# When the first layer's transfers are let go: pauses moved from POOL to DVE, key loads moved out of the norms' stages

## The chip, the cores and the metric

The kernel runs on one core of a Trainium2 chip. The core has five engines that run side by side, each its own list of instructions in order: PE (matrix products; its weight loads have their own row, PEld), DVE (element-wise work and reductions), ACT (activations and copies), POOL (further element-wise work) and SP, which here only issues DMA transfers. Engines wait for each other, and for transfers, through semaphores. The time that counts is the device time of one execution in microseconds, the median of several.

## The reference, cut to what matters

Two blocks follow each other: a delta-rule attention over 4 batches, 8 heads, 768 steps and 48 dimensions, and a feed-forward layer with a parametric ReLU over the 3072 tokens.

```python
k_n = k / (np.linalg.norm(k, axis=-1, keepdims=True) + 1e-06)
for t in range(S):
    kt, vt, bt = (k_n[:, :, t], v[:, :, t], beta[:, :, t, None])
    y[:, :, t] = np.einsum('bhd,bhde->bhe', q[:, :, t], state)
    v_old = np.einsum('bhde,bhd->bhe', state, kt)
    state = state + bt[:, :, :, None] * np.einsum('bhd,bhe->bhde', kt, vt - v_old)
...
x = np.ascontiguousarray(attn_out.transpose(0, 2, 1, 3)).reshape(B * S, H * D)
h = x @ w_in                                        # 3072 x 384 times 384 x 2048
g = np.maximum(h, 0.0) + alpha * np.minimum(h, 0.0)
return (g @ w_out).astype(np.float32)               # 3072 x 2048 times 2048 x 384
```

## The kernel before

**Steps.** The 768 positions are cut into 12 chunks of 64. A step n is one chunk of one pair of batches, so there are 24 steps; steps 2c and 2c + 1 are chunk c. Inside a step the recurrence over 64 positions becomes small products of 64 x 48 blocks: the Gram products of the keys (`grams`, L495), the triangular system they give, which steps 0 to 3 solve in rounds (`matrix`, `own_values`, `one_round`, all through L866) and later steps with an inverse made by elimination on DVE (`eliminate`), the outputs (`outputs`, L939) and the state's update (`next_state`, L955 and L963). `to_ffn` transposes a step's output (L978), and when both steps of a chunk are done the chunk goes through the two products of the feed-forward layer, first layer `ffn_in` (L1084, with ACT L1094 and DVE L1096 making the activation), second layer `ffn_out` (L1127).

**Weights.** Both weight matrices come as 8-byte numbers and are made into 4-byte ones on the chip, by the generator `weights` (from L203). `w_in` comes in 12 pieces of 128 x 512 numbers, 512 KB each. For a piece, SP issues the transfer into a staging area (L230), ACT makes two halves (L247, L249; `begin_half`), DVE shifts (L263) and POOL adds (L270). `begin_in(n)` has ACT begin all pieces up to n. The staging areas of pieces 0 to 5 lie in `w_out`, of 6 and 7 in `space_out`, 8 and 9 in `more`, 10 in `sums`, 11 in `turned`. The conversion fetches only the first four pieces by itself (`STAGED` is 4). Every later one is let go by a *pause*: a memset of one element of its staging area by some engine, for which SP must wait before it issues the transfer. So the pause's place in that engine's list sets the earliest time of the transfer:

```python
def pause(n, engine=nc.gpsimd):
    engine.memset(in_stages[n][0:1, 0:1].bitcast(FP32), 0.0)
    fetch_in(n + 1)
```

`pause_out` (L1697) does the same for the 128-row pieces of `w_out`, and `hold_v` (L165) lets a load of values wait for two one-element memsets of POOL.

**Keys.** `load_early(n)` (through L137) brings the keys of step n into one of three buffers; it can go when the earlier step in that buffer has been flipped (PE, L439) and squared (ACT, L395). `squared`, then `norms` (DVE, L402), `root` (ACT, L417 and L418), the reciprocal (DVE, L422) and two products of POOL (L428, L429) give a step's weights; all that follows the norms is `weigh`.

**Order.** The whole order is written out by hand: what a function emits goes to the end of its engine's list at that moment. The part around the change is `second_pair` (from L1814): it solves steps 2 and 3 (n and m, chunk 1), runs the first layer for chunk 0 beside it, converts the pieces of `w_in` from the fourth on and the first of `w_out`, and prepares the keys, norms and Grams of steps 4 to 7 (x is 4). `alongside(p, c)` mixes p parts of the first layer (a part is one 128-column product, two PE instructions) with c parts of the conversion (two to a piece). `burst(step, width)` emits a step of the solution for both n and m at once. The other places it names are `through_state` (L816, L804, then DVE L824 and L517), `turn_matrix` and `turn_values` (POOL, L882), `scale_first` (L854, by DVE for n and POOL for m), the weighting of the Grams by DVE (L503) and POOL's copy of part of it (L538).

Of the kernel before, what the change touches and what calls it, by code (L numbers as in the profile page):

```python
# [39 lines left out]
STAGED = 4  # L40
# [3 lines left out]
def kernel(  # L44
# [11 lines left out]
    nc = tc.nc  # L56
# [19 lines left out]
    def ps_big():  # L76

        big.append(big.pop(0))
        return big[-1]
# [24 lines left out]
    def half(i):  # L104
        return slice(64 * i, 64 * i + 64)

    def dims(i):
        return slice(64 * i, 64 * i + D)
# [14 lines left out]
    NKE, NKL, NQ = 3, 2, 2  # L123
# [5 lines left out]
    def early(n):  # L129

        return k_late[1] if n == NKE else k_early[n % NKE]

    def fetch(a, n, dst, queues=(nc.sync, nc.sync)):
        c, bp = steps[n]
        for t in range(2):
            src = a[2 * bp + t, :, c * C : (c + 1) * C, :].rearrange("h p d -> p h d")
            queues[t].dma_start(out=dst[half(t)], in_=src)  # L137

    def load_early(n, *queues):
        if n < N:  # L140
            fetch(k, n, early(n)[:, :, 0:D], *queues)
# [19 lines left out]
    def hold_v(n, engine=nc.gpsimd):  # L161

        v_raw[n] = work.tile([128, H, D], FP32, name="v_raw", bufs=3)
        for t in range(2):
            engine.memset(v_raw[n][64 * t : 64 * t + 1, 0, 0:1], 0.0)  # L165

    def load_v(n):
        if n < N:
            if n not in v_raw:
                v_raw[n] = work.tile([128, H, D], FP32, name="v_raw", bufs=3)  # L170
            fetch(v, n, v_raw[n])
# [237 lines left out]
    def weigh(n):  # L409
        if n >= N:  # L410
            return []
        norm = stats[n]
        root(norm)
        return [lambda: weigh_rest(n, norm)]

    def root(norm):
        nc.scalar.sqrt(norm, norm)  # L417
        nc.scalar.activation(norm, norm, ACT.Copy, bias=1e-6)  # L418

    def weigh_rest(n, norm):  # L420
        rec = work.tile([128, H], FP32, name="rec")
        nc.vector.reciprocal(rec, norm)  # L422
        weights_of(n, norm, rec)
# [48 lines left out]
    def quarters():  # L472
        return [(g, a, t) for g in range(G) for a in range(2) for t in range(2)]

    def now(pieces):
        for x in pieces:
            x()

    def region(p, n, **into):

        p = ps_big()[:, :, 0:n] if p is None else p
        assert p.shape[-1] == n
        return p.rearrange("p a (g i) -> p a g i", **into)

    def grams(n, p=None, u=0):

        if n >= N:
            return []
        if n < NJ:
            p = p.rearrange("p a (g u i) -> p a g u i", g=G, u=2)[:, :, :, u]  # L490
        else:
            p = region(p, G * C, g=G)
        for g, a, t in quarters():
            own = half(t ^ a) if n < NJ else half(t)
            nc.tensor.matmul(  # L495
                p[own, a, g], k_t[n][dims(a), g, half(t)], k_t[n][dims(a), g, half(t)]
            )
        if n < NJ:
            return p

        def weighted(dst, cols):
            w = stats[n][1][:, 0:2, :, None].to_broadcast([128, 2, G, HB])
            nc.vector.tensor_tensor(  # L503
                out=dst.rearrange("p (a g) i -> p a g i", a=2), in0=p[:, :, :, cols], in1=w,
                op=ALU.mult,
            )

        return [
            lambda: weighted(gather(n), slice(0, HB)),
            lambda: weighted(right[n % EARLY][:, 1:], slice(HB, C)),  # L510
            lambda: keep(n),
        ]
# [13 lines left out]
    def gather(n):  # L526
        m, j = n // NJ, n % NJ
        if j == 0:
            same[m] = work.tile([128, NJ, H, HB], FP32, name="same", bufs=1)
        return same[m][:, j]  # L530

    def keep(n):

        m, j = n // NJ, n % NJ
        for t in range(2):
            own = slice(64 * t + HB, 64 * t + C)
            if n < FIRST + NJ:
                nc.gpsimd.tensor_copy(out=same[m][own, j], in_=right[n % EARLY][own, 1:])  # L538
            else:
                nc.scalar.copy(same[m][own, j], right[n % EARLY][own, 1:])  # L540
# [901 lines left out]
    def part(gen, n):  # L1442
        for _ in range(n):
            next(gen, None)
            yield

    def weave(*gens):

        live = []
        for i, (g, n, *at) in enumerate(gens):  # L1450
            at = at[0] if at else 0.0
            live.append([at, i, (1.0 - at) / n, g])
        while live:
            live.sort(key=lambda x: (x[0], x[1]))
            at = live[0]
            at[0] += at[2]
            try:
                next(at[3])
            except StopIteration:
                live.pop(0)  # L1460
# [208 lines left out]
    n = 2 * W_IN_P  # L1669
# [13 lines left out]
# [4 lines that stand above are left out]
# [8 lines left out]
    def pause_out(n, engine=nc.vector):  # L1695

        engine.memset(out_stages[n][0:1, 0:1].bitcast(FP32), 0.0)  # L1697
        fetch_out(n + 1)
# [111 lines left out]
    def alongside(products, pieces, *gens):  # L1810
        gens = [(part(first_in, products), products), (part(convert_on, pieces), pieces), *gens]
        weave(*[x for x in gens if x[1] > 0])

    def second_pair():  # L1814

        n, m, x = 2, 3, NJ
        both = (n, m)

        def burst(step, width):
            p = ps_big()  # L1820
            pieces = []
            for i in range(2):
                pieces += step(n + i, p[:, :, i * width : (i + 1) * width])
            now(pieces)

        def keys(k):
            if k == x + 3:
                flip_more(k)
            squared(k)
            norms(k)  # L1830
            load_early(k + NKE)

        def through(i, p):
            now(through_state(i, None, p))

        now(next_state(0))
        hold_v(n)
        load_v(n)
        pause(STAGED + 2)
        alongside(2, 2)  # L1840
        now(next_state(1))
        keys(x)
        load_v(m)
        pause(STAGED + 3)
        alongside(3, 2)
        pause(STAGED + 4)
        burst(matrix, G * C)
        for i in both:
            turn_matrix(i, nc.gpsimd)
        now(weigh(x))  # L1850
        alongside(3, 2)
        scale_first(n, nc.vector)
        pause(STAGED + 5)
        scale_first(m)
        alongside(2, 0)
        keys(x + 1)
        begin_in(STAGED + 3)
        alongside(2, 1)
        y = ps_big()
        through(n, y[:, :, 0 : G * D])  # L1860
        alongside(2, 1)
        through(m, y[:, :, G * D : 2 * G * D])
        now(weigh(x + 1))
        pause(STAGED + 6)
        begin_in(STAGED + 4)
        alongside(2, 1)
        now(grams(x))
        begin_in(STAGED + 5)
        alongside(2, 2)
        ahead[0] = FT * DM  # L1870
        pause(STAGED + 7)
        burst(own_values, G * D)
        for i in both:
            turn_values(i, nc.gpsimd)
        alongside(2, 1)
        keys(x + 2)
        pause_out(0, nc.gpsimd)
        alongside(2, 2)
        pause_out(1, nc.gpsimd)
        now(grams(x + 1))  # L1880
        alongside(2, 1)
        burst(lambda i, p: one_round(i, 0, p), G * D)
        pause_out(2, nc.gpsimd)
        now(weigh(x + 2))
        alongside(2, 1)
        keys(x + 3)
        alongside(2, 1)
        now(grams(x + 2))
        alongside(2, 2)
        burst(lambda i, p: one_round(i, 1, p), G * D)  # L1890
        pause_out(3)
        now(weigh(x + 3))
        alongside(2, 1)
        now(grams(x + 3))
        alongside(2, 1)
        pause_out(4)
        burst(lambda i, p: one_round(i, 2, p), G * D)
        pause_out(5)
        alongside(3, 3, (part(blocks, 2), 2))
        burst(outputs, G * D)  # L1900
        pause_out(6)
        alongside(4, 3)
        for i in both:
            to_ffn(i)
        squares(x + 4)
        alongside(2, 1, (part(blocks, 2), 2))
        alongside(IN_PARTS - 43, 0, (part(blocks, 2), 2))

    def flip_more(n):
        now(flipped(n, ps_one()))  # L1910
# [21 lines left out]
    n = WHOLE + PIECES - BEGUN - SOON  # L1932
# [28 lines left out]
    n = OUT_PARTS - few - 2 * rest + 1  # L1961
# [54 lines left out]
    for n in range(JOINED, N):  # L2016
# [18 lines left out]
        m, ends = (n + 6) // NJ, n % NJ == 2  # L2035
# [57 lines left out]
```

## Time and profile before

| what | value |
|---|---|
| median of 3 runs | 648.46 us (647.12 to 650.54) |
| the profiled execution | 648.82 us, of which the span from first to last instruction 647.0 us |
| busy in the span: PE, DVE, ACT, POOL | 632.3, 484.4, 259.3, 125.0 us |
| mean granted clock of PE | 0.997 of full speed |
| PE busy from 40 to 60 us | 18.22 of 20 us, at clock 0.91 |
| PE busy from 60 to 80 and from 80 to 100 us | 20.00 and 19.67 of 20 us, at clock 1.00 |
| DMA share from 40 to 60 us | 0.74 of 16 engines, 188 GB/s |
| to landing: pieces of `w_in` into `w_out`, `space_out`, `more`, `sums`, `turned` | 4.8, 6.1, 6.0, 5.6, 4.0 us |

The page gives each engine's busy time in the whole execution; tables by stages give the same for stretches, with the clock that PE was granted and the share of time that the DMA engines were moving data. In a list of instructions a row holds start, duration, engine, line, operation, what is written from what, and how many in a row; in brackets stands how long the engine had been idle before, and what ended that. "issue" there means that the engine waited for nothing that the profile shows. In the view of transfers, q1 is the queue of SP's transfers, and the queues marked "instruction" bring the engines' own code.

### The profile page before, as it was taken

Reading aid. Unit: us, or ns where it says so; the run is one execution under the profiler, and the core shown is the slowest. Engines: PE = TensorE matmul, PEld = TensorE weight load, DVE = VectorE, ACT = ScalarE, POOL = GpSimd, SP = SyncE. Lnnn points to the kernel's source line nnn. Section 1 sums busy time; section 2 is a strip of 40 time slices with the busy share of each in tenths; the row PEclk is TensorE's granted clock in tenths of the full one; section 3 lists DMA queues with packets and bytes.
Section 4 is the critical chain, followed back from the end, with each engine's and each line's share of the span. In section 5 each row is a group of like instructions: output and inputs, shape, how many; then the busy total and the mean of one; then the engine's idle time right before and its main releaser. Section 6 shows DMA issues by size and latency. Waiting matters only on the chain.

```text
span 647.0 us, 21430 instructions
## 1 busy us (share of the span) xinstructions
PE 632.3 (98%) x9177; PEld 560.4 (87%) x9177; DVE 484.4 (75%) x1164; ACT 259.3 (40%) x605; POOL 125.0 (19%) x258
## 2 busy tenths in 40 slices
PE   7898999999999999999999999999999999999997
PEld 6577877566789989989989989989999999999997
DVE  6767889978998787578678578678878568477383
ACT  6675655145644253154144144033145054042240
POOL 8266611010001000000000010000043053062360
PEclk9998999999999999999999999999999999999999
DMA  7666685013511320321211111111120210100000
GB/s 122 176 152 202 204 178 133 15 37 63 100 22 32 77 45 7 60 41 27 54 29 21 40 38 25 39 39 27 38 50 15 54 23 2 40 2 2 25 0 26
DMA packets 106799, 36.89 MB, mean 57 GB/s; under 512 B 99872, under 2 KB 103088, under 8 KB 106704
## 3 DMA queue, kind: packets, MB, share of 16 engines
q1 hardware_dynamic: 104832, 35.03, 24.6%
q8 instruction: 72, 1.18, 0.7%
q10 hardware_dynamic: 1872, 0.49, 0.4%
q14 instruction: 23, 0.19, 0.1%
HBM read 30.78 MB, written 4.72 MB: 55 GB/s over the span
## 4 chain that ended last, share of the span: by engine, by line
PE 86%; DVE 6%; DMA 2%; POOL 2%; issue 2%; ACT 1%; SPq 0%; POOLq 0%; DVEq 0%; ACTq 0%
PE p_ffn L1084 22%; PE p_ffn L1149 17%; PE p_more L1401 8%; PE p_ffn L1127 5%; PE p_more L1317 5%; PE p_ffn L1307 3%; PE p_ffn L1401 3%; PE p_pair L816 3%; PE p_ffn L1312 2%; PE p_pair L756 2%; PE p_pair L439 2%; PE p_pair L939 2%; PE p_pair L926 2%; PE p_pair L804 1%; PE p_pair L495 1%
## 5 line engine op out<-in xcount | busy, mean ns | idle before, releaser
L1084 PE MATMUL p_ffn<-xt,w_in 128*128 128x256 f32 x768 | 178.3, 385 | 0.9 <-DVE act L1096 0.5
L1084 PEld LDWEIGHTS p_ffn<-xt,w_in 128*128 128x128 f32 x768 | 142.2, 190 | 21.9 <-issue 1.7
L1094 ACT ACTIVATE act<-p_ffn 128x512 f32<-128x512 f32 x56 | 33.4, 596 | 80.5 <-PE p_ffn L1084 80.3
L1096 DVE SCALAR_TENSOR_TENSOR act<-act,al_t,p_ffn 128x256 f32<-128x256 f32 x112 | 48.6, 475 | 22.3 <-ACT act L1094 22.1
L1341 POOL TENSOR_TENSOR k_t<-k_t 128x128 f32<-128x128 f32 (+1 forms) x48 | 29.5, 614 | 165.9 <-ACT k_t L1336 163.4
L580 DVE TENSOR_TENSOR block<-block,prod 128x30 f32<-128x30 f32 (+9 forms) x150 | 50.0, 333 | 5.1
L574 DVE TENSOR_TENSOR prod<-block 128x30 f32<-128x30 f32 (+9 forms) x150 | 49.1, 328 | 4.2 <-POOL block L564 2.8
L428 POOL TENSOR_TENSOR beta_t<-beta_t,rec 128x8 f32<-128x8 f32 x20 | 5.1, 254 | 235.5 <-DVE rec L422 219.7
L1149 PE MATMUL p_ffn<-w_out,act 128*128 128x192 f32 x288 | 49.6, 328 | 0.0
L1149 PEld LDWEIGHTS p_ffn<-w_out,act 128*128 128x128 f32 x288 | 46.5, 190 | 0.3
L982 ACT COPY xt<-p_pair 128x384 f32<-128x384 f32 x22 | 10.4, 479 | 90.6 <-PE p_pair L978 76.8
L1341 POOL TENSOR_TENSOR block<-block 128x128 f32<-128x128 f32 (+1 forms) x48 | 28.2, 587 | 17.0 <-ACT block L1336 14.5
L1307 PE MATMUL p_ffn<-xt,w_in 128*128 128x256 f32 x96 | 28.7, 380 | 0.0
L768 ACT COPY inv<-p_pair 32x256 f32<-32x256 f32 x40 | 14.5, 362 | 25.0 <-DVE u L930 24.2
L808 ACT COPY y<-p_pair 128x384 f32<-128x384 f32 x22 | 10.5, 479 | 32.8 <-PE p_pair L804 31.2
L1169 DVE TENSOR_TENSOR o_sb<-u,p_ffn 128x192 f32<-128x192 f32 x24 | 7.9, 351 | 20.5 <-PE p_ffn L1149 20.0
L1355 DVE SCALAR_TENSOR_TENSOR act<-block,al_t,act 128x256 f32<-128x256 f32 x32 | 19.1, 636 | 5.4 <-ACT block L1351 5.4
L834 DVE TENSOR_TENSOR r<-v_raw,p_pair 64x192 f32<-64x192 f32 (+1 forms) x60 | 21.2, 353 | 1.1
L1401 PE MATMUL p_more<-w_out,act 128*128 128x192 f32 x128 | 21.9, 329 | 0.0
L816 PE MATMUL p_pair<-beside,k_t 48*64 48x112 f32 x704 | 21.5, 259 | 0.2 <-ACT beside L467 0.2
L963 DVE TENSOR_TENSOR beside<-beside,p_pair 48x384 f32<-48x384 f32 (+1 forms) x38 | 20.9, 549 | 1.0 <-PE p_pair L955 0.8
L1336 ACT COPY k_t<-p_more 128x512 f32<-128x512 f32 x16 | 9.4, 586 | 30.3 <-PE p_more L1317 25.6
(292 smaller groups left out, 1412.0 us busy)
## 6 DMA issues: line engine op xcount, KB each, us to landing
v_raw<-in_v_dram SPq DMA_DIRECT2D x48, 96.0 KB, 2.9
qp<-in_q_dram SPq DMA_DIRECT2D x48, 96.0 KB, 3.0
out_dram<-o_sb SPq DMA_DIRECT2D x90, 48.0 KB, 1.6
space_out<-in_moe_w_out_dram SPq DMA_DIRECT2D x11, 384.0 KB, 3.7
ke<-in_k_dram SPq DMA_DIRECT2D x43, 96.0 KB, 3.3
kl<-in_k_dram SPq DMA_DIRECT2D x80, 48.0 KB, 2.5
w_out<-in_moe_w_in_dram SPq DMA_DIRECT2D x6, 512.0 KB, 4.8
w_out<-in_moe_w_out_dram SPq DMA_DIRECT2D x5, 384.0 KB, 3.4
```

What stands on the lines that cost most here:

```text
L574: nc.vector.tensor_tensor(out=prod, in0=r[:, 0:j, j : j + 1].to_broadcast([128, j, n]), in1=r[:, j : j + 1, j + 1 : HB].to_broadcast([128, ...
L580: nc.vector.tensor_tensor(out=r[:, 0:j, j + 1 : HB], in0=r[:, 0:j, j + 1 : HB], in1=prod, op=ALU.add)
L816: nc.tensor.matmul(p[half(t ^ a), a, g], k_t[n][dims(a), g, half(t)], beside[bp][dims(a), t, g])
L1084: nc.tensor.matmul(p_h[:, i], w_in[:, t, (f + i) * 128 : (f + i + 1) * 128], xt[:, t], start=(t == 0), stop=(t == KT - 1),)
L1094: nc.scalar.activation(g, p_h, ACT.Relu, scale=-1.0)
L1096: nc.vector.scalar_tensor_tensor(out=g[:, i], in0=g[:, i], scalar=al_t[:, f + i : f + i + 1], in1=p_h[:, i], op0=ALU.mult, op1=ALU.add,)
L1127: nc.tensor.matmul(p_o[u], gs[f // 2][:, f % 2, u * 128 : (u + 1) * 128], w_out[:, f], start=(f == 0), stop=(f == FT - 1),)
L1149: nc.tensor.matmul(p, x(i), w(i), start=(i == 0), stop=(i == FP - 1))
L1307: nc.tensor.matmul(p[:, f * 256 : f * 256 + 256], w(2, f), xt[:, 2], start=True, stop=False)
L1317: nc.tensor.matmul(q[:, j], a, b, start=True, stop=True)
L1341: nc.gpsimd.tensor_tensor(out=dst, in0=a, in1=b, op=ALU.add)
L1401: nc.tensor.matmul(p, x(i), w(i), start=(i == 0), stop=(i == FP - 1))
```

## The change

It touches only `second_pair`.

- Both value loads, with a hold each, are emitted at the start; before, the second came without a hold behind the first key load.
- The pause for piece 6 (`STAGED + 2`) stays on POOL and goes behind the norms of step 4. The pauses for pieces 7 to 11 go to DVE: behind the weights of step 4, behind DVE's `scale_first`, behind the weights of step 5, behind the Grams of step 4, and behind the own values.
- `keys` no longer loads the next keys. The four loads (steps 7 to 10) are emitted behind the norms of step 5, behind the own values, and behind the third and the fourth pause of `w_out`.

```diff
             squared(k)
             norms(k)
-            load_early(k + NKE)
...
         now(next_state(0))
-        hold_v(n)
-        load_v(n)
-        pause(STAGED + 2)
+        for i in both:
+            hold_v(i)
+            load_v(i)
         alongside(2, 2)
         now(next_state(1))
         keys(x)
-        load_v(m)
-        pause(STAGED + 3)
+        pause(STAGED + 2)
         alongside(3, 2)
-        pause(STAGED + 4)
         burst(matrix, G * C)
         for i in both:
             turn_matrix(i, nc.gpsimd)
         now(weigh(x))
+        pause(STAGED + 3, nc.vector)
         alongside(3, 2)
         scale_first(n, nc.vector)
-        pause(STAGED + 5)
+        pause(STAGED + 4, nc.vector)
         scale_first(m)
         alongside(2, 0)
         keys(x + 1)
+        load_early(x + NKE)
         begin_in(STAGED + 3)
...
         now(weigh(x + 1))
-        pause(STAGED + 6)
+        pause(STAGED + 5, nc.vector)
         begin_in(STAGED + 4)
         alongside(2, 1)
         now(grams(x))
+        pause(STAGED + 6, nc.vector)
         begin_in(STAGED + 5)
         alongside(2, 2)
         ahead[0] = FT * DM
-        pause(STAGED + 7)
         burst(own_values, G * D)
+        load_early(x + NKE + 1)
+        pause(STAGED + 7, nc.vector)
         for i in both:
             turn_values(i, nc.gpsimd)
...
         pause_out(2, nc.gpsimd)
+        load_early(x + NKE + 2)
         now(weigh(x + 2))
...
         pause_out(3)
+        load_early(x + NKE + 3)
         now(weigh(x + 3))
```

## The prediction

> **What bounds the kernel now.** I read the profile's page first, for the bound.
>
> ```profile
> span 647.0 us, 21430 instructions
> PE 632.3 (98%) x9177; PEld 560.4 (87%) x9177; DVE 484.4 (75%) x1164; ACT 259.3 (40%) x605; POOL 125.0 (19%) x258
> ...
> q8 instruction: 72, 1.18, 0.7%
> ```
>
> PE is the bound, so a change in the first layer is worth only PE's idle time and slow clock there. Code is data too: 1.18 MB in 72 packets is 16.4 KB a packet, and 18,354 PE instructions over 72 packets make about 255 each, some 128 matmuls with their weight loads. Next, PE's instructions in order of time, from 50 us, where the change acts.
>
> ```profile
> 51.65 0.50 PE L495 MATMUL p_pair<-k_t 48*64 48x64 f32 x17
> 53.93 0.46 PE L495 MATMUL p_pair<-k_t 48*64 48x64 f32 x15 [1.78 <-issue]
> 54.31 1.62 PE L1084 MATMUL p_ffn<-xt,w_in 128*128 128x256 f32 x4
> 55.86 1.96 PE L866 MATMUL p_pair<-r,diag 64*64 64x48 f32 x64
> ```
>
> One burst of 32 Gram products is cut in two by 1.78 us in which PE waits for no semaphore. From 40 to 100 us it is PE's only gap but one (0.33 at 86.26). The table by stages (PE, PEld, DVE, ACT, POOL busy, then the granted clock, DMA share, GB/s) gives the rest of its price.
>
> ```profile
> 52.00:54.00 2.00, 0.22 (x14) 0.14 (x9) 1.46 (x4) 1.94 (x4) 0.51 (x3) 1.00 0.79 154
> 54.00:56.00 2.00, 2.00 (x23) 1.21 (x26) 0.76 (x2) 0.12 (x2) 0.63 (x2) 0.71 0.53 126
> 56.00:58.00 2.00, 2.00 (x65) 1.91 (x66) 1.36 (x4) 1.97 (x4) 1.48 (x3) 0.50 0.39 152
> 58.00:62.00 4.00, 4.00 (x72) 3.05 (x75) 2.94 (x7) 1.89 (x4) 3.20 (x7) 0.97 0.72 186
> ```
>
> The clock lost is 2 x 0.29 + 2 x 0.50 + 4 x 0.03 = 1.70 us, so the hole costs 1.78 + 1.70 = 3.48 us at most. Two stretches of the DMA view say what it waits for: 47.4 to 51.3 first, 51.3 to 52.6 second.
>
> ```profile
> q1 hardware_dynamic: 345, 1.18, 90.4%
> ```
> ```profile
> q1 hardware_dynamic: 549, 0.39, 95.6%
> q8 instruction: 1, 0.02, 4.9%
> ```
>
> In the first stretch data fill the engines and no code packet runs; one runs in the second (4.9% of 16 x 1.3 us is 1.02 us), and PE goes on 1.5 us later. I read it as code behind two pieces issued at 46.55 and 48.18 and a key load at 48.60. The chain that ended last says what a gain there would meet:
>
> ```profile
> 64.85 0.43 ACT ksq L395
> 65.28 0.02 issue
> 65.31 0.50 DVE norm L402
> ...
> 71.68 0.04 DVE w_out L1697
> 71.71 0.02 issue
> 71.73 3.56 DMA w_out<-in_moe_w_out_dram
> ...
> 85.57 0.88 DVE sums L1096 x2
> 86.45 0.14 issue
> 86.59 2.83 PE p_ffn L1084 x12
> ```
>
> From 65.31 to 86.45 the chain runs through DVE, POOL, ACT and one DMA, and not through PE. DVE's list marks only 0.88 us of waiting between 65.8 and 77 (0.60 at 70.51, 0.28 at 76.57). If only PE gets earlier, it waits at 86.
>
> **The change part by part.** Pieces 6 to 11 of the first layer's weights are those let go by the six pauses, STAGED+2 to STAGED+7.
>
> *Memsets.* Five pauses go from POOL (89 ns each, 0.45 us) to DVE (59 ns in the row of the later pauses, 0.30 us). DVE's idle 0.98, 1.40 and 1.02 us before 54.44, 56.60 and 60.73 hide that; without them it is +0.30. POOL gains two holds of v_raw, 0.18 us.
>
> *Second value load.* From 42.52 to about 39.6, behind the first. POOL reads it at 48.18 after 1.7 us of DVE's matching work: no gain.
>
> *Piece 6.* Issued at 39.60, now behind POOL's sum at 40.26 to 41.56: 41.6. The pieces land 4.0 to 7.2 us after issue, so 45.6 to 48.8; ACT takes it at 45.83. At most 3 us late, it is covered by ACT's idle 0.56 and 1.97 us before 48.28 and 50.73 and by DVE, which comes to that ACT output only at 50.07; I take nothing.
>
> *Piece 7.* From 43.93 to DVE's reciprocal at 44.99: 45.3, landing by 52.5 at worst, wanted at 51.46. With the usual 4 to 6 us it is in time.
>
> *Piece 8.* From 46.55 to the end of DVE's scaling, 48.96: 49.0, landing 53.0 to 56.2, wanted 52.73. I take 53.2, as the queue is empty before it: ACT waits 0.5 us, and behind it on ACT stands an activation (55.97) that has 1.89 us of idle ahead.
>
> *Keys.* The load at 41.19 goes to 49.4 (first used by the flip at 63.63); that of 48.60 to about 55; the next two go behind three and four pieces of w_out. No load of keys waits for a late square any more, and what stands on SP behind a pause that waits for DVE is at most the next key load, used 8 us later or more. The load put behind w_out's fourth piece shares the engines with the fifth, whose landing stands in the chain: 0 to 1.3 us (a pair issues for 1.28), and I take 0, because the fifth waits for its own memset.
>
> *The hole.* From 41 to 52 us the value load, two key loads and three pieces are issued before; now three pieces and one key load, of which 45.3 to 49.0 has one piece. 128 matmuls back from the gap (64 in 50 to 52, 64 of the 104 in 46 to 50) is about 47.5; if PE asks for code one packet ahead, it does so there, and now meets nearly free engines. I take the hole as gone: own_values on PE start at 55.86 - 1.78 - 0.49 (four matmuls 1.62 instead of 1.13) = 53.6 and end at 54.7 (1.16 at full clock in the row at 42.30).
>
> *Pieces 9 to 11, where the gain meets them.* Piece 9 moves from 48.18 to DVE's reciprocal at 52.98: 53.3, landing about 57.5; ACT wanted it at 56.87 and would now want it near 55. In ACT's order behind it stand pieces 10 (53.86 before, 54.7 now, landing 59.2 against 59.5) and 11 and the next activation. Piece 11: DVE's Gram weighting cannot start before POOL's weights at 53.80; then 0.75 + 0.87 + 0.46 + 1.0 us of DVE to the end of the own values, 57.0, memset, issue at 57.2 against 57.60. Landing after the same 4.0 us is 61.2 against 61.6. Before, from its conversion (61.73) to the end of round 0 on DVE (64.75) took 3.0 us; now that ends at 64.3. DVE's norm then starts at 64.5 instead of 65.31, for the key flip that held it, 63.63 on PE, has become earlier with the hole. From there the chain is the old one: 0.8 us earlier at 86.59.
>
> Sum: PE gains up to 3.48, and gives back 2.7 in waits at rounds 1 and 2, the outputs and 86; the net is -0.8 us. The profiled execution took 648.82 (span 647.0 and 1.8 around it); 648.0 in its terms. The median shown is 648.46, and against that I say 647.6.
>
> [...] The table shows 1.70 us of clock lost after 1.78 us of idleness. [...]
>
> **The rivals.**
>
> *All of it stays.* If the chain of 65 to 86 has more slack than I read, or piece 11 lands faster, PE keeps 3.48: 645.0. Against it: DVE's last output sum ends at 76.0 and PE's transposes of it start at 76.01, so PE has none to spare there.
>
> *The hole stays.* If the code packet does not stand behind the data, PE still stops at 52.15, and the pieces are only later: the own values end at 58.91, piece 11 is issued at 59.05 instead of 57.60, lands 1.45 later, and DVE's 0.45 us of idleness before 65.31 covers part: +1.0, 649.5. For it: no view shows when the packet was asked for. [...] No code packet in 3.9 us of 90% load speaks against it.
>
> *The last piece lands late, and PE waits as long as before* (slower). PE comes to round 1 at about 63.6 if the hole is gone, and round 0 ends 3.1 us after piece 11 lands. From a landing at 62.3 on (5.1 us after issue, where rows of this stage have 4.0 to 7.2) that wait is 1.78 us, long enough for the clock to fall, 1.70. At 62.3: 0.65 + 1.70 = +2.35, 650.8; at 64.4: +2.8 + 1.7 = +4.5, 653.0. For it: keys now stand between pieces 10 and 11, and a late piece 8 delays the own values. Against: the queue is emptier.
>
> **How the numbers follow.** Forecast 0.52, all stays 0.18, hole stays 0.10, late piece 0.20. A measurement here can tell about 0.5%, 3.2 us, from no change. Faster by more: 0.16 of "all stays" and 0.03 of the forecast, 0.19. Slower: 0.16 of the late piece and 0.02 of the forecast, 0.18. Within: 0.63. The range runs from 644.9, just under "all stays", to 651.6, in the middle of the late piece's 650.8 to 653.0, which leaves about 0.06 below and 0.11 above. The unknown landings alone (4.0 to 5.1) would give 646.8 to 648.9.
>
> **What would show it.** Right: no gap inside the Gram burst near 52, clock 1.00 from 54 to 62, a code packet before 50.5; piece 11 issued near 57.2; new waits of PE for DVE at rounds 1 and 2 and near 86 that add up to 2 to 3 us. Wrong: the hole still at the same 18th product, or another of 1.5 us or more with the clock at 0.50 behind it; or a first conversion that ACT waits over 2 us for.

## The result, and the profile after

The median after the change is 650.1 us (649.04 to 655.09, 22 executions), against 648.4 us (646.31 to 651.74, 22 executions) of the kernel before on the same chips: a ratio of 1.0029 with a 95% interval of 1.0016 to 1.0043. The change makes the kernel slower by 0.3%, about 1.9 us. The profiled execution took 651.51 us, 2.69 more than that of before.

The page of the changed kernel, for what PE did in all:

```profile
span 649.8 us, 21438 instructions
...
PE 635.4 (98%) x9177; PEld 563.2 (87%) x9177; DVE 483.8 (74%) x1169; ACT 259.1 (40%) x605; POOL 123.7 (19%) x255
```

PE's instructions in order of time, columns as before:

```profile
41.45 0.55 PE L955 MATMUL p_pair<-u,kl 64*64 64x48 f32 x18 [0.96 <-issue]
...
52.61 0.69 PE L495 MATMUL p_pair<-k_t 48*64 48x64 f32 x32
...
67.47 0.68 PE L866 MATMUL p_pair<-mid,act 64*64 64x48 f32 x32 [3.16 <-DVE sums L921]
```

The Gram burst is whole: its 32 products stand in one row, where before it was cut by 1.78 us. A stop of the same kind, without a semaphore, is now at 40.49 (0.96 us). PE has its 1100th product 2.60 us earlier than before (57.75 against 60.35). Then it waits 3.16 us for DVE ahead of round 1, and the table by stages (PE, PEld, DVE, ACT, POOL busy, then clock, DMA share, GB/s) shows what follows:

```profile
66.00:68.00 2.00, 0.53 (x36) 0.53 (x38) 2.00 (x7) 2.00 (x5) 0.25 (x2) 1.00 0.79 214
68.00:70.00 2.00, 2.00 (x48) 1.47 (x40) 1.91 (x6) 1.94 (x6) 1.94 (x3) 0.70 0.05 11
70.00:72.00 2.00, 2.00 (x34) 1.45 (x34) 1.33 (x5) 1.15 (x3) 1.88 (x4) 0.50 0.00 0
```

The half clock has moved with the idleness, from 54.8 to 58.2 before to 68.8 to 72.2 now. From 82 us on every product is 2.8 to 2.9 us later than before, to the end: all of the difference is made in the first 82 us.

Why DVE is late stands in three lists. SP's issues (start, duration) first:

```profile
54.32 0.33 SPq L230 DMA_DIRECT2D more<-in_moe_w_in_dram  x1
55.33 0.84 SPq L230 DMA_DIRECT2D sums<-in_moe_w_in_dram  x1
56.27 1.28 SPq L137 DMA_DIRECT2D ke<-in_k_dram  x2
58.88 0.33 SPq L230 DMA_DIRECT2D turned<-in_moe_w_in_dram  x1
```

ACT's first halves of these three pieces (9, 10, 11), each with what ended ACT's idle time:

```profile
58.33 0.68 ACT L247 ACTIVATE w_in<-more 128x512 uint32<-128x512 uint32 x1 [1.45 <-DMA more<-in_moe_w_in_dram]
...
62.25 0.68 ACT L247 ACTIVATE w_in<-sums 128x512 uint32<-128x512 uint32 x1 [2.52 <-DMA sums<-in_moe_w_in_dram]
...
64.44 0.66 ACT L247 ACTIVATE w_in<-turned 128x512 uint32<-128x512 uint32 x1 [0.81 <-DMA turned<-in_moe_w_in_dram]
```

And DVE behind them:

```profile
63.66 0.43 DVE L263 TENSOR_SCALAR sums<-sums 128x512 uint32<-128x512 uint32 x1 [2.72 <-ACT sums L249]
65.62 0.87 DVE L1096 SCALAR_TENSOR_TENSOR act<-act,al_t,p_ffn 128x256 f32<-128x256 f32 x2 [1.53 <-ACT act L1094]
...
66.87 0.55 DVE L921 TENSOR_TENSOR sums<-sums,p_pair 128x384 f32<-128x384 f32 x1
```

The same two places before, from ACT's list (the first half of piece 11) and from DVE's (the end of round 0):

```profile
61.73 0.69 ACT L247 ACTIVATE w_in<-turned 128x512 uint32<-128x512 uint32 x1 [0.80 <-POOL w_in L270]
```
```profile
64.20 0.55 DVE L921 TENSOR_TENSOR sums<-sums,p_pair 128x384 f32<-128x384 f32 x1
```

Pieces 9, 10 and 11 land 3.9, 6.8 and 5.5 us after their issues. ACT waits 4.78 us in all for them; the activation of the first layer (L1094, at 65.00) stands on ACT behind piece 11, and on DVE the shift of piece 10 and the products of that activation stand ahead of round 0 (L921). So round 0 ends on DVE at 67.42 (66.87 and 0.55) instead of 64.75, 2.67 us later, about the 2.8 at the end. The chain that ended last runs through that transfer:

```profile
58.88 5.47 DMA turned<-in_moe_w_in_dram
...
64.44 0.66 ACT w_in L247
```

### The profile page after: what moved, and what is told of

Its sections match the earlier page's. It is cut to its first block, busy times and chain, and to the rows that moved or that the text cites. A ratio compares the mean times of both kernels' runs of the same rounds, so it can differ in the third digit from the quotient of the medians.

```text
span 649.8 us, 21438 instructions
## 1 busy us (share of the span) xinstructions
PE 635.4 (98%) x9177; PEld 563.2 (87%) x9177; DVE 483.8 (74%) x1169; ACT 259.1 (40%) x605; POOL 123.7 (19%) x255
## 4 chain that ended last, share of the span: by engine, by line
PE 83%; DVE 9%; DMA 3%; ACT 3%; issue 2%; POOL 1%; DVEq 0%; ACTq 0%; POOLq 0%
PE p_ffn L1084 21%; PE p_ffn L1149 17%; PE p_more L1401 8%; PE p_ffn L1127 5%; PE p_more L1317 5%; PE p_ffn L1307 3%; PE p_ffn L1401 3%; PE p_ffn L1312 2%; PE p_pair L756 2%; PE p_pair L816 2%; PE p_pair L439 2%; PE p_pair L939 2%; PE p_pair L926 2%; PE p_pair L495 1%; PE p_pair L804 1%
## 5 line engine op out<-in xcount | busy, mean ns | idle before, releaser
L1094 ACT ACTIVATE act<-p_ffn 128x512 f32<-128x512 f32 x56 | 33.3, 594 | 78.5 <-PE p_ffn L1084 78.3
L1355 DVE SCALAR_TENSOR_TENSOR act<-k_t,al_t,act 128x256 f32<-128x256 f32 x32 | 21.7, 718 | 0.1
```

The costliest lines, as they stand in the source:

```text
L1094: nc.scalar.activation(g, p_h, ACT.Relu, scale=-1.0)
L1355: nc.vector.scalar_tensor_tensor(out=g[:, f], in0=r[:, f], scalar=al_t[:, 2 * i + f : 2 * i + f + 1], in1=g[:, f], op0=ALU.mult, op1=ALU.add,)
```

## The experiments

Ratios are to the kernel before on the same chip, with 95% intervals of some 0.15 to 0.2% to either side; two variants that ran on one chip can also be set against each other, by the means of their executions, to about 1 us (0.15%). Smaller differences are not resolved. "Wait" is PE's idleness ahead of round 1 in the profiled execution, with the clock behind it. Landings are counted from the issue of the piece. The last column, like the wait, is of one execution, and need not show what the median shows: e12 stands there at +0.03 us, though its ratio comes to some 1.7 us.

| kernel | ratio | piece 10: issue, landing | piece 11: issue, landing | wait, us | PE's delay against the first execution of before, at 93 us |
|---|---|---|---|---|---|
| after | 1.0029 [1.0016, 1.0043] | 55.33, +6.8 | 58.88, +5.5 | 3.16, half | +2.87 |
| after, a second execution (a2) | | 54.74, +5.9 | 58.29, +4.9 | 2.39, full | +1.75 |
| before, the first execution | | 53.86, +5.6 | 57.60, +4.0 | 0 | 0 |
| before, a second execution (b2) | | 52.88, +3.8 | 55.53, +6.0 | 2.33, half | -0.66 |
| before, a third execution (b3) | | 54.60, +3.9 | 57.55, +4.6 | 1.26, full | +0.02 |
| e1: pieces 9 to 11 back | 1.0009 [0.9991, 1.0027] | 53.97, +4.7 | 56.91, +4.4 | 0.98, full | -0.26 |
| e2: keys alone | 1.0006 [0.9988, 1.0025] | 52.35, +3.9 | 55.01, +6.4 | 2.71, half | -0.08 |
| e3: pauses alone | 1.0029 [1.0013, 1.0046] | 55.29, +4.6 | 58.84, +4.4 | 1.87, half | +0.89 |
| e9: pauses 9 to 11 alone | 1.0019 [1.0001, 1.0038] | 53.68, +5.6 | 57.23, +5.9 | 2.76, full | +0.82 |
| e12: pauses 6 to 8 alone | 1.0026 [1.0013, 1.0039] | 53.18, about +4 | 56.42, +6.0 | 2.54, full | +0.03 |
| e16: after, piece 9 back | 1.0025 [1.0007, 1.0043] | 53.94, +5.3 | 57.50, +5.4 | 2.96, half | +2.23 |

**One half of the change at a time (e2, e3).** e2 is the kernel before with the key loads alone moved (the first line is in `keys`):

```diff
-            load_early(k + NKE)
...
         keys(x + 1)
+        load_early(x + NKE)
...
         burst(own_values, G * D)
+        load_early(x + NKE + 1)
...
         pause_out(2, nc.gpsimd)
+        load_early(x + NKE + 2)
...
         pause_out(3)
+        load_early(x + NKE + 3)
```

> The kernel before with only the four key loads moved; value loads and all six pauses as before. Theory L with the reading of the hole as code behind data: two key loads (1.3 us of all engines each) are gone from the 41 to 52 us stretch, the hole at 52 shrinks to under 0.5 us or goes, pieces land as before, no wait at round 1 over 0.7 us: 645.5 to 647.5 against 648.4. Rival P (the pieces alone fill the engines, keys do not matter): hole of 1.5 us or more stays, 648 to 649.

e3 is the kernel before with the six pauses alone moved, the two diffs of e9 and e12 below together; key and value loads stay as they were.

> The kernel before with only the pauses moved (piece 6 behind the norms, 7 to 11 on DVE); value loads and key loads as before. Theory L: the wait at round 1 is there (2 to 4 us) with a fall of the clock, the hole at 52 is gone, 649.5 to 651. Rival K (the key loads' new places delay the last pieces): wait at round 1 under 1 us, 646 to 648.

Measured: keys alone 1.0006 [0.9988, 1.0025], pauses alone 1.0029, the whole of the loss. The two ran on one chip, and there the mean of e3 is 1.6 us above that of e2 (95%: 0.6 to 2.5). In both the stop inside the Gram burst is missing. With the keys alone PE is 4.98 us ahead at its 1100th product and hands nearly all of it back: 2.71 us of waiting ahead of round 1, then half clock, and 0.08 us are left at 93 us. e3 came out as its theory L said, but for a wait that is a little short (1.87). Neither theory for e2 held: the hole is gone, as theory L said, but the wait that it ruled out is there, and the kernel is not faster.

**Which pauses (e1, e9, e12, e16).** e9 is the kernel before with the pauses of pieces 9, 10 and 11 alone moved, and e1 the changed kernel with the same edit taken back:

```diff
-        pause(STAGED + 5)
         scale_first(m)
...
         now(weigh(x + 1))
-        pause(STAGED + 6)
+        pause(STAGED + 5, nc.vector)
...
         now(grams(x))
+        pause(STAGED + 6, nc.vector)
...
-        pause(STAGED + 7)
         burst(own_values, G * D)
+        pause(STAGED + 7, nc.vector)
```

> The changed kernel with the pauses of pieces 9, 10 and 11 back on POOL at their old places; values, keys and pieces 6 to 8 stay as changed. Theory L (the loss is PE's wait of 3.16 us for round 0 and the 1.70 us of half clock behind it, because the last three pieces are let go too late): no wait of PE before round 1 over 0.7 us, full clock from 66 to 74 us, 4 to 5 us faster than the changed kernel's 650.1, so 645 to 646; if the code hole at 52 us comes back because piece 9 is early again, 3.5 of that is lost, 648.5 to 649.5, and the hole is seen. Rival S (the loss comes from the start of the stage, both value loads first and PE's gap of 0.96 us at 41): about as the changed kernel, 649.5 to 650.5.

> The kernel before with one part of the change alone: the pauses of pieces 9, 10 and 11 on DVE at their new places, those of 6 to 8 and all key loads as before. Theory A (what the change costs is that pieces 9 to 11 are let go later): ratio 1.002 to 1.003, piece 11 issued after 58 us, and PE waits 1.5 to 3 us for DVE before round 1. Rival (it is the moved key load between pieces 10 and 11, or the earlier pauses): ratio 0.999 to 1.001 and no wait of over 1 us there.

e12 moves the pauses of pieces 6, 7 and 8 alone:

```diff
-        pause(STAGED + 2)
         alongside(2, 2)
...
-        pause(STAGED + 3)
+        pause(STAGED + 2)
         alongside(3, 2)
-        pause(STAGED + 4)
...
         now(weigh(x))
+        pause(STAGED + 3, nc.vector)
...
         scale_first(n, nc.vector)
+        pause(STAGED + 4, nc.vector)
         pause(STAGED + 5)
```

> The kernel before with the pauses of pieces 6, 7 and 8 alone at their new places; those of 9 to 11 stay on POOL where they were, and the key loads too. Theory A (only the late let-go of pieces 9 to 11 costs): ratio 0.999 to 1.001. Rival (the later pieces 6 to 8 cost as much): ratio 1.002 to 1.003, and ACT waits over 1 us for piece 8 or 9.

e1 measured 1.0009: taking the three late pauses back takes, by the middle values, most of the loss away (on the same chip e3 and e4 are on the mean 1.3 and 1.0 us above it, each to about 1.1 us), and PE's wait falls to 0.98. Theory L's 645 to 646, a gain over the kernel before, did not come. e9 gave 1.0019, so the three alone bring a part of it. But e12, which theory A had at 0.999 to 1.001, gave 1.0026, the rival's number, though not in the rival's way: ACT does not wait for pieces 8 and 9 but for 10 (1.33 us) and for 11, ahead of which it is idle for 3.65 us. Piece 11, issued at 56.42, took 6.0 us to land. So "only the late pauses cost" fell. e1 moved the same three pauses and the keys besides; that it is better by 0.17% is not resolved. What the costly kernels share is the landing of piece 11: between 62.4 and 64.4 us in the profiled execution of every one with a ratio of 1.0019 or more (after, e3, e4, e9, e12, e13, e16), at 61.3 and 61.4 in e1 and e2, and 61.5 to 62.2 in the three executions of before. PE comes to round 1 at 61.8 to 64.5 us in all of them but the first execution of before. This is association. In e12 and e13 the profiled execution does not show the loss at all (PE is 0.03 and 0.29 us late at 93 us), and what their slower executions do was not profiled, so where e12's loss arises stays open.

e16 tests whether piece 10 lands late because it is issued 1.0 us behind piece 9: the changed kernel with piece 9 alone back on POOL.

```diff
         pause(STAGED + 4, nc.vector)
+        pause(STAGED + 5)
         scale_first(m)
...
         now(weigh(x + 1))
-        pause(STAGED + 5, nc.vector)
```

> The changed kernel with piece 9 alone let go by POOL at its old place, pieces 10 and 11 by DVE as changed. Theory A (the largest single loss is piece 10, issued 1.0 us behind piece 9 and so landing 5.6 to 6.8 us after issue): piece 10, now alone, lands in 3.9 to 4.8 us, before 59.5; ACT waits under 1 us for it; the wait of PE before round 1 falls to 0.5 to 1.8 us, as piece 11 is still issued near 58; ratio 1.000 to 1.002. Rival (the code packet that falls among the pieces decides, not their spacing): piece 10 still takes 5.5 us or more, the wait stays at 2.2 us or more, ratio 1.003.

ACT's first halves of pieces 10 and 11 in e16:

```profile
59.31 0.68 ACT L247 ACTIVATE w_in<-sums 128x512 uint32<-128x512 uint32 x1 [2.68 <-DMA sums<-in_moe_w_in_dram]
...
63.03 0.66 ACT L247 ACTIVATE w_in<-turned 128x512 uint32<-128x512 uint32 x1 [2.32 <-DMA turned<-in_moe_w_in_dram]
```

Piece 10 was issued 4.7 us behind piece 9 and landed in 5.3, between both theories' numbers; the wait stayed at 2.96 and the ratio at 1.0025. Theory A falls. Spacing may have its part (issued 1.0 us behind piece 9, piece 10 took 5.6 to 6.8 us in the changed kernel, e5, e9 and e13, but 4.6 in e3 and at most 4.4 in e4), but it does not decide. Piece 11 was issued only 0.59 us later than in e1 and landed 1.7 us later.

**Does the late landing act through the order of the lists (e5 to e8)?** The conversion of pieces 10 and 11 is put behind round 0, in the changed kernel (e5), in e2 (e6), in the kernel before (e7) and in e1 (e8):

```diff
-        ahead[0] = FT * DM
...
         now(grams(x + 1))
-        alongside(2, 1)
+        alongside(2, 0)
         burst(lambda i, p: one_round(i, 0, p), G * D)
+        ahead[0] = FT * DM
...
         now(weigh(x + 2))
-        alongside(2, 1)
+        alongside(2, 2)
```

> The changed kernel with the conversion of pieces 10 and 11 begun behind round 0 instead of ahead of it (DVE's shift of piece 10, and ACT's first halves of 10 and 11); transfers as changed. Theory O (PE's 3.16 us before round 1 come from the order: ACT waits for pieces 10 and 11 with the activation that round 0's additions stand behind, and DVE's shift of piece 10 stands in front of them): wait before round 1 under 0.5 us, no fall of the clock there, 2 to 4 us faster than the changed kernel, 646 to 648. Rival D (the last pieces are late wherever they stand): the wait only moves, to the first layer's products that need pieces 9 to 11 behind round 2, or to the outputs; PE waits 2 us or more there, 649 to 650.5.

> The kernel before with only the key loads moved, and the conversion of pieces 10 and 11 behind round 0. Theory O: PE keeps a good part of the 5 us that it was ahead of the kernel before at round 1 in the run with the key loads alone: 1 to 3 us faster than before, 645 to 647 against 647.8. Rival D, or the chain through DVE from 65 to 86 us binds whatever comes before it: within 0.7 us of before.

> The kernel before with only the conversion of pieces 10 and 11 moved behind round 0. Both theories: the hole at 52 us stays (1.5 us or more), there was no wait at round 1 to lose, DVE does the same work; within 0.7 us of before, and where the chain through DVE from 65 to 86 us binds, not better. It tells what of the next two runs is the order alone.

> The changed kernel with the pauses of pieces 9 to 11 back at their old places and the conversion of 10 and 11 behind round 0. Theory O: waits of PE at round 1 and at 78 us (0.98 and 1.28 without the new order) fall under 0.5 each, 645 to 647. Rival D or the chain binds: 647.5 to 649.

PE in e5:

```profile
63.55 0.68 PE L866 MATMUL p_pair<-mid,act 64*64 64x48 f32 x32
...
68.81 0.68 PE L866 MATMUL p_pair<-r,act 64*64 64x48 f32 x32 [1.36 <-DVE r L921]
...
80.45 0.67 PE L1084 MATMUL p_ffn<-xt,w_in 128*128 128x256 f32 x2 [1.68 <-ACT act L1094]
```

The pieces land as late as in the changed kernel (10 in 6.1 us at 60.7, 11 in 5.0 at 63.2), yet round 1 starts with no wait: that wait came from their conversion standing ahead of round 0. Much as rival D said, the waiting moved, to round 2 and to 80 us, 3.04 us together. Ratios: e5 1.0008 [0.9992, 1.0024], e6 1.0001 [0.9983, 1.0019], e7 0.9998 [0.9981, 1.0015], e8 1.0001 [0.9988, 1.0015]. So by the middle values the order takes away most of the changed kernel's loss (1.0029 to 1.0008; the intervals overlap), and in e5, e7 and e14 below, where the conversion stands behind round 0, a piece 11 that lands at 62.9 to 63.8 goes with ratios of 0.9998 to 1.0008. It gains nothing over the kernel before, and theory O's faster times for e5, e6 and e8 did not come: what PE keeps at round 1 it waits at round 2 (0.39 to 1.36 us) and near 78 us (0.35 to 1.83 us), for ACT and DVE. In e7 the hole at 52 us, which both theories had staying, is missing.

**The keys (e4, e10, e13, e14).** e4 is the changed kernel with the key load between pieces 10 and 11 put behind the third pause of w_out:

```diff
-        load_early(x + NKE + 1)
         pause(STAGED + 7, nc.vector)
...
         pause_out(2, nc.gpsimd)
+        load_early(x + NKE + 1)
         load_early(x + NKE + 2)
```

> The changed kernel with the one key load that stands between pieces 10 and 11 put behind the third pause of w_out. Theory K: piece 11, and with it the wait at round 1, comes 1.3 us or more earlier, wait 1 to 2 us, 647.5 to 649. Theory L: piece 10 (issued at 55.33, taken at 62.25) was late before that load could matter, the wait at round 1 falls by less than 0.7 us, 649.5 to 650.2.

It measured 1.0027 [1.0010, 1.0045], with a wait of 1.52 and a stop of 1.16 us without a semaphore at 70.38: no help. The wait is theory K's, the time theory L's; piece 11 was issued at 58.80 instead of 58.88, so the key load was not what delayed its issue. e13 takes the other two key loads of the changed kernel out of w_out's pieces:

```diff
         pause_out(2, nc.gpsimd)
-        load_early(x + NKE + 2)
...
         pause_out(3)
-        load_early(x + NKE + 3)
...
         pause_out(6)
+        load_early(x + NKE + 2)
+        load_early(x + NKE + 3)
```

> The changed kernel with one edit: the last two key loads go behind w_out's sixth pause instead of its third and fourth. Theory A (the late pieces 9 to 11 set round 1 and everything behind it, so w_out's transfers are not what ends last): ratio to the kernel before 1.001 to 1.003, the wait before round 1 still 1.5 us or more. Rival (the key loads among w_out's pieces carry the loss): ratio 0.998 to 1.000.

It measured 1.0040 [1.0020, 1.0061], just past theory A's 1.001 to 1.003, with a wait of 2.15: these loads do not carry the loss. e10 is e8 with the same edit, and e14 is e10 again.

> The changed kernel with pieces 9 to 11 let go by POOL at their old places, their conversion begun behind round 0, and now the last two key loads put behind w_out's sixth pause instead of its third and fourth. Theory A (behind 60 us the chain goes through w_out's transfers, and the key loads among them delay it): the wait of PE at the second layer near 78 us, 1.58 us without this edit, shrinks to under 0.8 and the ratio comes to 0.997 to 0.999. Rival (the chain there goes through DVE's and ACT's own work): that wait stays at 1.2 to 1.9 us, and the ratio stays at 1.000.

> The version that was fastest so far, measured again: the changed kernel with pieces 9 to 11 let go by POOL at their old places, their conversion begun behind round 0, and the last two key loads behind w_out's sixth pause. If 0.9979 was no accident: 0.996 to 0.9995, no wait of PE over 1 us between 40 and 90 us, span 644.5 to 646. If it was: 0.9995 to 1.001.

PE in e10:

```profile
67.83 0.68 PE L866 MATMUL p_pair<-r,act 64*64 64x48 f32 x32 [0.28 <-DVE r L921]
...
78.23 0.67 PE L1084 MATMUL p_ffn<-xt,w_in 128*128 128x256 f32 x2 [0.45 <-DVE act L1096]
```

The waits shrank as theory A said (1.58 to 0.45 near 78), and e10 measured 0.9979 [0.9959, 0.9999]. The second time it measured 1.0003 [0.9989, 1.0017]. A gain of 0.2% is not confirmed; no version is shown to beat the kernel before. e13 and e14 ran on one chip and differ in pieces 9 to 11 alone, in who lets them go and in where the last two are converted: the mean of e13 is 2.8 us above that of e14 (95%: 1.6 to 4.0), so the loss comes with these two together.

**The stop in the Gram burst (a2, b2, b3, e11).** b2 and b3 are further executions of the kernel before, a2 one of the changed kernel, all without an edit.

> The kernel before, unchanged, looked at a second time. Theory A (the stop of PE inside the Gram burst belongs to the kernel: code stands behind SP's transfers whenever these are let go as before): a gap of 1.5 us or more at PE instruction 1985 (7.75 blocks of 256), clock 0.50 behind it, span near 647. Theory B (it is a matter of one execution: PE's code comes in time or not by where the packet falls among the transfers): the gap can be missing; then PE is about 3.5 us ahead at its 1100th product and waits 1 to 3 us for DVE between 62 and 80 us, and the span is again 646 to 648.

> The kernel before, unchanged, looked at a third time. Theory A (the stop in the Gram burst and the wait before round 1 take each other's place, since piece 11's landing sets the end): either a stop of PE of 0.5 to 2 us near instruction 1985 and under 0.5 us of waiting before round 1, or no stop and 1.5 to 3 us of waiting there; span 646 to 648 in both cases. Rival (the two are independent): both or neither.

> The changed kernel, unchanged, looked at a second time. Theory A (pieces 9 to 11 are let go too late by DVE's own work, in every execution): no stop of PE inside the Gram burst, piece 11 issued at 58 to 59, ACT idle over 2 us before one of the pieces 10 and 11, and PE waits 1.5 us or more for DVE before round 1. [...] Rival (the wait of 3.16 us was a matter of one execution): under 1 us of waiting there.

PE in b2, in two stretches:

```profile
50.52 0.80 PE L495 MATMUL p_pair<-k_t 48*64 48x64 f32 x32
```
```profile
64.67 0.94 PE L866 MATMUL p_pair<-mid,act 64*64 64x48 f32 x32 [2.33 <-DVE sums L921]
```

The stop is not there. Nor is it in b3, nor in e7, where the transfers are let go as before. So its absence from the changed kernel cannot be put down to the change. In its place PE waits 2.33 and 1.26 us ahead of round 1 in b2 and b3, and the spans are 646.3 and 647.0 us against 647.0 with the stop. So in these three executions the stop of 1.78 us and its half clock cost 0 to 0.7 us at the end, not 3.48. That is theory B for b2; in b3 the wait is shorter than theory A's 1.5, and e9 has both a stop there (0.70 us) and a wait (2.76), so that the one does not rule the other out. b3 also has a stop of its own, where the changed kernel has its stop of 0.96 us at 40.49:

```profile
41.09 0.55 PE L955 MATMUL p_pair<-u,kl 64*64 64x48 f32 x18 [1.23 <-issue]
```

This one is missing in 4 of the 20 executions profiled (the first two of before, e7, e16) and 0.41 to 1.51 us long in the others. So it too goes by the execution, and is not shown to come from the change. The changed kernel's wait came again (2.39), with round 1 late again.

e11 puts two more transfers of 512 KB, whose data nothing uses, behind the issue of piece 9 of the kernel before:

```diff
         pause(STAGED + 5)
+        for i in range(2):
+            nc.sync.dma_start(out=in_stages[i], in_=moe_w_in[128 * i : 128 * i + 128, 0:W_IN_P].bitcast(U32))
```

> The kernel before with two extra transfers of 512 KB each, into the staging areas of pieces 0 and 1, which are long converted, right behind the issue of piece 9 (work that the output does not need). Theory A (PE's code stands behind the data that SP has issued): some 5 us of transfers more stand ahead of the code packet, and the stop inside the Gram burst grows to 3 us or more, or a stop of that size comes elsewhere between 48 and 58 us; pieces 10 and 11 land 4 us later and PE waits over 3 us before round 1 as well. Rival (the code packet takes its turn with the data, and the stop had another cause): no gap of PE over 2 us before round 1, only the late pieces.

PE in e11:

```profile
59.63 0.62 PE L866 MATMUL p_pair<-act 64*64 64x48 f32 x28 [0.71 <-issue]
```

A stop did come, later and smaller (0.71 us at 58.92, not 3), and pieces 10 and 11 landed later than in b3 (61.1 and 63.1 against 58.5 and 62.2). PE waits 1.41 us before round 1, not over 3. The trace's packets, set beside PE's instructions (matrix products, weight loads and PE's own semaphore instructions, some 130, in order of start), tell more. From 38 to 98 us (packets 5 to 13) code packet k starts near the moment when PE starts its instruction 256k, from 1.4 us ahead of it to 3.55 us behind it; where PE stops for it, it stops near instruction 256k + 192. In the profile of before packet 7 starts at 51.42, the 1792nd instruction at 47.88, and the stop runs from 52.15 to 53.93. All stops of 0.4 us or more without a semaphore, from 38 us on and in 20 executions, lie at 5.76, 7.75, 8.75 or 10.75 times 256 instructions, and PE goes on 1.3 to 1.6 us after that packet's end. Packet 7 came 3.55 us behind the 1792nd instruction where the stop of 1.78 is, with the engines 94% busy with data in that time, and 2.48 behind it in e9 (a stop of 0.70); at most 1.74 in all others, without a stop there. Packet 8 of e11 came 2.81 us behind its instruction, at 97%; at most 1.6 elsewhere. The author reads these stops as waits for code that came late; in e9 and e11 the stop was 1.8 and 2.1 us shorter than the packet's delay. That the code was late because data stood ahead of it fits these three packets, with theory A's size wrong. It is not shown: e11 is one execution, and packet 5 came up to 3.48 us late (e13) with data in 72% of the engines' time meanwhile. The measure of 256 instructions is read from the traces: in the profiles of before and after the stops of 0.4 us or more without a semaphore, from 28 us on, come ahead of PE's instructions 962, 1218, 1474 and 1985, which lie one or two times 256 apart to within one, and 72 code packets of 16.4 KB go with 18,488 instructions of PE, 257 each.

**What makes piece 11 late.** The DMA view over the 2.5 us behind the issue of piece 11, in e2 and then in e1 (queue, packets, MB, share of 16 engines; then the issue with its landing):

```profile
q1 hardware_dynamic: 128, 0.47, 62.9%
q8 instruction: 1, 0.02, 2.6%
...
turned<-in_moe_w_in_dram SPq DMA_DIRECT2D x1, 512.0 KB, 6.4
```
```profile
turned<-in_moe_w_in_dram SPq DMA_DIRECT2D x1, 512.0 KB, 4.4
```

In e2 a code packet starts 2.28 us behind the issue, in e1 none until 4.07. Over the 20 executions: in the ten where a packet starts 0.9 to 2.3 us behind the issue of piece 11, it lands in 4.9 to 6.4 us; in nine of the other ten in 3.8 to 4.9, and in e11, with its extra data, in 5.5. This is association, and its limits were set after the fact: packets 0.71 and 0.83 us behind the issue, in e13 and b3, go with landings in 4.4 and 4.6. When a code packet comes goes with where PE is: a PE that has not stopped in the Gram burst comes to the instruction of packet 9 earlier (at 57 to 60.5 us instead of 62), while the pieces are under way; the packet starts at 61.88 before, with that instruction at 62.05, and at 60.28 after the change, with it at 59.45. That the packet itself holds the piece up was not tried by itself, and stays open.

## Why the prediction was wrong

The prediction had 647.6 us and most likely no change; the time is 650.1, inside its range of 644.9 to 651.6 and inside the 0.5%. But the forecast was 0.8 us faster, the kernel is about 1.9 us slower, and what happened is its rival "the last piece lands late". Two of its own signs of being wrong are there: a new idleness of over 1.5 us with half clock behind it (3.16 us), and a first conversion that ACT waits over 2 us for (2.52, piece 10).

- *The hole* is gone as forecast, the packet at 49.60 (before 50.5, as named), PE ahead by 2.60 us, about the 3.48 less the stop of 0.96 at 40.49. But b2, b3 and e7 lack the hole without the change, so that the emptier queue is not shown to be the reason: this part may have come right by luck. The stop at 40.49, which was not foreseen, put pieces 7 to 9 a microsecond late: 46.35, 50.17, 54.32 against 45.3, 49.0, 53.3.
- *What the hole was worth* was taken from one execution. The two further executions of the kernel before are without it, and end no more than 0.7 us earlier.
- *Memsets, second value load, piece 6* held: 60 ns each beside other work; 39.54; issued at 41.54 (41.6).
- *"Pieces 9 to 11, where the gain meets them"* is the step that failed, by its dates of issue and landing. Piece 10 was to land 4.5 us after its issue and took 6.8, though the row of piece 9 in the profile of before (7.2 us, issued 1.6 behind piece 8) was the nearest to a piece issued 1.0 us behind another. Piece 11 was to be issued at 57.2, 4.0 to landing: 58.88 and 5.5. Of the 1.7 us of issue, 1.0 goes with the stop at 40.49 (in a2, where it is 0.41, the issue is at 58.29), and the rest with DVE's 1.22 us of idleness before 56.50, behind an ACT that had waited for piece 8. Round 0 was to end at 64.3 and ended at 67.42. Why the two pieces took so long to land stays open.
- *The rival's mechanism* is what happened, though the key load between pieces 10 and 11, which it named as a reason, was not what delayed piece 11's issue (e4). Its price for a landing at 64.4 was +4.5, of which 1.70 for the clock. The profiled execution has +2.7. In these executions the clock's part does not reach the end: in a2 the clock stays full and PE is still 1.75 late, and in b2 it falls and PE ends 0.66 early. From 64 to 86 us the chain is not PE's, as the prediction said of gains; the same holds of losses.
- *The chance* of 0.20 for it rested on "against: the queue is emptier", which looked at data only. In the profiled execution a code packet of 1.82 us ran from 60.28, and pieces 10 and 11 landed behind it; whether it delayed them is not shown.
- *"The last output sum leaves no slack"*, against "all of it stays", held in the main: of leads of 1.6 to 5 us at the 1100th product no variant kept over 1.5 past 93 us.

## What to carry to other kernels

A stall of the busiest engine is worth its removal only if the next hand-over to that engine is early too: find, for the place where the gain is to arrive, the last input that it waits for, and date that one from the slowest comparable row. A transfer let go later should have its new landing dated from a row with the same neighbours in the queue, code packets among them (piece 10 was dated at 4.5 us here and took 6.8), and where its conversion stands ahead of critical work in an in-order list, moving the conversion was safer here than moving the transfer. Before a stall of a microsecond or two is costed, profile the unchanged kernel more than once.

## What the hardware showed that was not expected

In the traces of before and after the changes of PE's clock lie whole multiples of 3.41 us apart, however the idleness lies: at 54.82 and 58.24 before, at 14.18, 17.60, 68.80 and 72.21 after. Nor does the length of a gap alone tell whether the clock falls behind it. The clock fell behind gaps of 1.78 (before), 1.87 (e3), 2.33 (b2), 2.71 (e2), 2.96 (e16) and 3.16 us (after) and stayed full behind others of 2.39 (a2), 2.54 (e12) and 2.76 (e9). Of e9 the table by stages:

```profile
64.00:66.00 2.00, 0.00 (x0) 0.00 (x0) 1.62 (x4) 1.97 (x6) 0.00 (x0) 1.00 0.76 293
66.00:68.00 2.00, 1.76 (x67) 1.66 (x68) 1.91 (x7) 1.97 (x5) 1.48 (x3) 1.00 0.23 54
```

PE does nothing for all of the first 2 us, and the clock is 1.00 behind it. That a gap costs clock or not by where it lies among the steps of 3.41 us was the author's reading; what decides is not shown.
